# A written-out order of operations replaced by another one, in an attention and MLP-mixer kernel

## The chip, the cores and the metric

One core of one Trainium2 chip. The metric is the device time of one execution in microseconds (us). Each core has five engines with instruction queues of their own: TensorE (PE in the profile; its weight loads are listed as PEld), VectorE (DVE), ScalarE (ACT), GpSimd (POOL) and SyncE (SP). Transfers (DMAs) are issued from such a queue and run on the core's 16 DMA engines.

## What is computed

Sliding-window attention with a linear bias, whose output goes through an MLP-mixer layer. Shapes: q, k, v are (8, 8, 576, 64), the output is (8, 576, 512), all float32.

```python
# attention: B = 8, H = 8, S = 576, D = 64, window 128
scores = scale * np.matmul(q, k.transpose(0, 1, 3, 2))
rel = pos[:, None] - pos[None, :]
mask = (rel >= 0) & (rel < window)
scores = np.where(mask, scores + bias[None], -1000000000.0)   # bias: -slope(head) * |rel|
attn = softmax(scores)
x = np.matmul(attn, v)          # -> (8, 576, 512), heads side by side
# mixer: d_tok = 256, d_ch = 1536
h = np.maximum(x.transpose(0, 2, 1) @ w_tok1, 0.0) @ w_tok2
u = x + h.transpose(0, 2, 1)
h2 = np.maximum(u @ w_ch1, 0.0) @ w_ch2
out = u + h2
```

## The kernel before

**Tiling.** A sequence of 576 rows is four blocks of 128 and a rest of 64. Two batches form a pair; their rests share one tail block (block 8; blocks 0 to 3 are the first batch's, 4 to 7 the second's). Data is bfloat16 on the chip, float32 in the accumulators and in the output. All weights stay on the chip.

**Stages of a block and of a batch**, with the lines by which the profile names them:

- *Loads.* `load` (line 596) issues from POOL one transfer with conversion to bfloat16 per block and tensor, into rings of five `qk` and five `v` buffers. The tail block has two per tensor, one for each batch.
- *Turns.* q and k must stand with the head dimension on the partitions. `transposes` does that on PE (line 754, copied out at line 760) for the first pair's blocks and by a DMA transpose from SP (line 743) for the others, into a ring of seven `qkT` buffers.
- *Scores.* Matmuls of line 791, exp on ACT (line 806), mask multiplication on DVE (line 816). *Values:* matmuls of line 871 with a column of ones for the row sums, reciprocal on DVE (line 901), normalization on DVE (line 904) or ACT (line 909).
- *Token mix* (lines 933 to 994): two products with the token weights and the residual; the result `ub` is turned on PE for the first three batches and by SP's DMA transposes (line 1002) for the later ones.
- *Channel mix.* The first product is direct (line 1491) for batches 0 to 2 and in seven partial products (line 1391) for batches 3 to 7. Some of these seven are kept in float32 in buffers of the ring `ob` (named `raw` or `ob` in the profile; copy on ACT, line 1406, or on DVE, line 1407), later added to another product (line 1415) and cut at zero (DVE, line 1417, or ACT, line 1419). DVE prepares differences of the inputs at line 1354. The tail block has a direct product (line 1534).
- *Second product of the channel mix* (line 1668), again in seven partial products; the evictions (line 1639) add the residual into `ob` buffers, and line 1651 stores each finished quarter of a batch: from SP, but for batches 5 and 6 from POOL. The tail blocks have a product of line 1579, an eviction (line 1586) and two stores (line 1595).

While PE does the channel mix of batch b, the attention and the token mix of batch b + 1 run between its products: the kernel is one stream in which the stages of two batches are woven together.

**What sets the order.** The functions named above do not emit instructions. Each makes an operation (`Plan.op`) with its engine, its dependencies and the buffers it makes and uses; 1528 operations in all. Three constants written out at the head of the file then say what becomes of them, and `Plan.follow` reads them:

- `ORDER` (line 343): the numbers of the operations in base 36, in one sequence. Each engine executes its own operations in this sequence; there is no other priority.
- `ELSEWHERE` (line 388): operations that can run on ACT or DVE and are to run on the other one than their default.
- `PLACES` (line 391): for each buffer, in the order of first use, the slot of its ring (for `ps`, the PSUM bank). An operation that takes over a slot waits for all users of the slot's previous buffer.

```python
ops, seq = self.ops, [self.ops[number(x)] for x in ORDER.split()]
...
for x in ELSEWHERE.split():
    o = ops[number(x)]
    o.eng, o.cost, o.emit = o.other
line = {e: [o for o in seq if o.eng == e] for e in ("PE", "ACT", "DVE", "POOL", "SP")}
...
places = iter(PLACES)
for o in seq:
    for b in o.bufs:
        if b.slot is None:
            first = number(next(places))
```

The rest of `follow` only guesses times, by which `emit` sorts the operations (engine by engine this is the sequence of `ORDER`) and puts small matmuls of zeros (line 1726) into PE's guessed gaps of the first 60 us. The queues are in order: an instruction that waits holds all that stand behind it on its engine. POOL's queue holds the loads, one pause (line 1025, a small copy that waits for a turned block of batch 4) and the late stores; SP's holds both kinds of turns and the other stores.

Of the kernel before, what the change touches and what calls it, by code (L numbers as in the profile page):

```python
# [70 lines left out]
class Plan:  # L71
# [60 lines left out]
    def follow(self):  # L132
        def number(x):
            return int(x, 36)

        ops, seq = self.ops, [self.ops[number(x)] for x in ORDER.split()]
        assert sorted(o.n for o in seq) == list(range(len(ops)))
        for x in ELSEWHERE.split():
            o = ops[number(x)]
# [5 lines left out]
        for o in ops:  # L145
            for d in o.deps:
                succ[d].append(o)
        places = iter(PLACES)
        for o in seq:
# [134 lines left out]
    def emit(self, spin):  # L284
# [20 lines left out]
        for _, _, go in sorted(work, key=lambda w: w[:2]):  # L305
# [37 lines left out]
ORDER = ("h i 4z f j g 52 k d e 0 l 59 7 1 2 8 4v m 3 4 4x n 4w 9 4y o a 55 5 41 50 42 56 43 53 57 44 51 p 58 54 5c q "  # L343
# [44 lines left out]
ELSEWHERE = ("4w 4y 56 5m 63 6i 71 74 82 86 8a a1 a5 b4 b6 c1 c3 ct cz fb fo ft fw gh gj gn gp gr gt gv h7 j0 j2 jk jw ku "  # L388
             "l5 ls lu m0 n8 na of oo op oz qa qd qq qv qy sl t3 t6 th uc uf uh us vd vi vn wv y0 y2 z5 zx 10a 10f 125 12m "
             "12p 130 13n 13q 144 14e 14h 14w 154")  # L390
PLACES = ("000232243674016170016710104526473452324062714260014501022423400510303647106542202567210123732010446005172042"
          "362051274206715214600503123154312004710320646027513140700140215467140010640713055567102605442020611541127230"
          "025262104700230014425051403512010500312141045110243012320140672042576220135742000764034632027316250001410345"
          "032144211356403132100450246021001275130420276110007602714237320407630130523116201136100600423450014031202753"
          "010221310424602240716150473245124022651103414372613403103250016362440743151304001632203241351701025422040305"
          "000654201226422044020117553524030170503214160073144603151242005002361430470201452220764207205106323324401126"
          "21054020440646533020470006402521147105523572030164250114")
UNIT_LATE = False
SECOND_LATE = False
GATE = True  # L400
# [1360 lines left out]
```

## Time and profile before

| | us |
|---|---|
| runs of the kernel | 274.78, 274.56, 272.98 |
| median of them | 274.56 |
| the profiled execution's own time | 274.01 |
| its span on the core | 272.1 |
| granted TensorE clock | 1.00 |

The profile shows one execution. The span runs from the first to the last recorded activity; the profiled execution's own time is 1.9 us longer. "Busy" is the time that an engine spends in instructions; the matmuls' ends are modelled, and those of consecutive matmuls overlap, so distances from start to start are the safer measure of PE's pace. A wait is written as the instruction that waited and, behind the arrow, what came last before it could go, with the total, the number and the longest of such waits. In timeline rows the first two columns are start and length in us, and a wait that ended with the row's start stands in brackets. Of a DMA the row on POOL or SPq is the issue alone; a source view gives the time from issue to landing.

### The profile page before, as it was taken

The page shows a single profiled execution, that of the slowest core. Times are in us where ns is not written, and L with a number is a line of the kernel's source. Part 1 is how long each engine was busy: PE and PEld are TensorE (multiplying, and loading weights), DVE is VectorE, ACT ScalarE, POOL GpSimd, SP SyncE. Part 2 cuts the span into 40 slices and gives each one's busy share as a digit, 9 for nine tenths or more (in the row PEclk, how much of TensorE's full clock was granted, in tenths as well). Part 3 has the DMA queues.
Part 4 walks back from the last instruction along what each step waited for, and adds up shares of the span by engine and source line. Part 5 has one row for each costly group of instructions (what it writes and reads, how often), then busy time and mean ns, then how long its engine had stood idle before and what let it go on. Part 6 is the DMA issues. An engine that isn't in the chain of part 4 may idle for free.

```text
span 272.1 us, 7520 instructions
## 1 busy us (share of the span) xinstructions
PE 263.2 (97%) x3033; PEld 195.6 (72%) x3033; DVE 234.0 (86%) x533; ACT 159.5 (59%) x306; POOL 114.8 (42%) x147
## 2 busy tenths in 40 slices
PE   7989999999999999999999999999899989999994
PEld 5767565776686656588877876688776768588883
DVE  7886598983996799889999899999899989987992
ACT  6974787144963469229991299428881379413900
POOL 8987977640680866601680137400740410003000
PEclk9999999999999999999999999999999999999999
DMA  8999999999999999999999899979999430044006
GB/s 197 179 170 181 150 191 183 149 111 181 190 142 169 176 139 230 161 116 232 80 177 149 221 141 78 124 183 164 147 165 111 129 107 2 12 88 149 8 0 193
DMA packets 160338, 38.59 MB, mean 142 GB/s; under 512 B 146544, under 2 KB 159472, under 8 KB 160304
## 3 DMA queue, kind: packets, MB, share of 16 engines
q0 software_dynamic: 109968, 19.64, 90.3%
q1 hardware_dynamic: 49104, 17.70, 33.9%
q10 hardware_dynamic: 1232, 0.79, 1.0%
q8 instruction: 23, 0.38, 0.6%
q14 instruction: 11, 0.09, 0.1%
HBM read 35.85 MB, written 9.44 MB: 166 GB/s over the span
## 4 chain that ended last, share of the span: by engine, by line
PE 71%; DMA 11%; issue 7%; DVE 5%; POOL 4%; ACT 1%; SPq 0%; POOLq 0%; DVEq 0%
PE ps L1668 24%; PE ps L1391 11%; PE ps L1491 11%; PE ps L871 5%; PE ps L933 4%; PE ps L976 4%; PE ps L791 3%; DMA qk<-in_k_dram 3%; PE ps L1534 3%; PE ps L1579 3%; DMA v<-in_v_dram 2%; DMA qkT<-qk 2%; DMA W<-in_moe_w_tok_dram 2%; POOL qk L596 2%; DVE r L1415 2%
## 5 line engine op out<-in xcount | busy, mean ns | idle before, releaser
L806 ACT ACTIVATE pe<-ps 128x1024 bf16<-128x1024 f32 (+1 forms) x56 | 51.8, 971 | 15.8 <-PE ps L791 15.8
L596 POOL DMA_DIRECT2D qk<-in_k_dram x35 | 29.9, 868 | 52.2 <-DMA qkT<-qk 49.0
L596 POOL DMA_DIRECT2D v<-in_v_dram x36 | 30.9, 867 | 30.8 <-PE ps L871 29.9
L1668 PEld LDWEIGHTS <-r 128*128 128x128 bf16 x384 | 36.6, 98 | 8.0 <-issue 1.3
L596 POOL DMA_DIRECT2D qk<-in_q_dram x35 | 30.3, 875 | 11.4 <-DMA qkT<-qk 7.6
L816 DVE TENSOR_TENSOR pe<-pe,mask 128x1024 bf16<-128x1024 bf16 (+1 forms) x48 | 30.3, 647 | 3.4 <-ACT pe L806 3.2
L1491 PE MATMUL ps<-uT,WC 128*128 128x512 bf16 x132 | 32.0, 379 | 0.0
L1406 ACT COPY raw<-ps 128x512 f32<-128x512 f32 x32 | 19.0, 596 | 21.8 <-PE ps L1391 11.9
L1668 PEld LDWEIGHTS <-s 128*128 128x128 bf16 x288 | 27.7, 98 | 5.2 <-issue 0.4
L909 ACT ACTIVATE xb<-ps,rt 128x64 bf16<-128x64 f32 x80 | 18.3, 324 | 19.2 <-DVE rt L901 19.1
L1415 DVE TENSOR_TENSOR r<-ps,raw 128x512 bf16<-128x512 f32 x37 | 24.6, 679 | 1.8 <-PE ps L1391 1.7
L1391 PE MATMUL ps<-tt,WS 128*128 128x256 bf16 x180 | 25.9, 273 | 0.0
L1668 PE MATMUL ps<-WC,r 128*128 128x256 bf16 x192 | 25.7, 273 | 0.0
L1391 PEld LDWEIGHTS <-WS 128*128 128x128 bf16 x240 | 21.9, 98 | 4.9 <-issue 1.2
L871 PEld LDWEIGHTS <-pe 128*128 128x128 bf16 (+1 forms) x480 | 20.4, 99 | 6.5 <-issue 1.4
L1668 PE MATMUL ps<-WT,r 128*128 128x256 bf16 x192 | 24.7, 273 | 0.0
L1668 PE MATMUL ps<-WT,s 128*128 128x256 bf16 x192 | 24.1, 273 | 0.0
L871 PE MATMUL ps<-v,pe 128*128 128x65 bf16 (+1 forms) x480 | 23.0, 194 | 0.6 <-ACT pe L806 0.3
L994 DVE TENSOR_TENSOR ub<-ps,xb 128x512 bf16<-128x512 f32 x32 | 21.0, 683 | 2.9 <-PE ps L976 2.7
L1497 ACT ACTIVATE r<-ps 128x512 bf16<-128x512 f32 x26 | 15.1, 613 | 10.0 <-PE ps L1491 8.7
L1639 DVE TENSOR_TENSOR raw<-ps,ub 128x512 f32<-128x512 f32 x27 | 18.3, 683 | 2.1 <-PE ps L1668 2.1
L1491 PEld LDWEIGHTS <-WC 128*128 128x128 bf16 x132 | 11.6, 98 | 11.8 <-issue 0.2
(145 smaller groups left out, 519.1 us busy)
## 6 DMA issues: line engine op xcount, KB each, us to landing
out_dram<-raw SPq DMA_DIRECT2D x19, 256.0 KB, 2.6
qk<-in_q_dram POOLq DMA_DIRECT2D x30, 128.0 KB, 4.9
qk<-in_k_dram POOLq DMA_DIRECT2D x30, 128.0 KB, 4.9
v<-in_v_dram POOLq DMA_DIRECT2D x28, 128.0 KB, 5.6
WC<-in_moe_w_ch_dram POOLq DMA_DIRECT2D x8, 384.0 KB, 7.6
out_dram<-raw POOLq DMA_DIRECT2D x8, 256.0 KB, 2.8
out_dram<-ob SPq DMA_DIRECT2D x5, 256.0 KB, 2.6
v<-in_v_dram POOLq DMA_DIRECT2D x16, 64.0 KB, 4.8
```

What stands on the lines that cost most here:

```text
L596: nc.gpsimd.dma_start(out=to()[p0 : p0 + n, :, :], in_=rows(src, b, s0, n))
L806: act_.activation(out=pb()[:, e, :, lo:, c0:c1_], in_=wide(e)[:, :, lo:, c0:c1_], func=ACT.Exp, scale=scale)
L816: dve_.tensor_tensor(out=o, in0=o, in1=heads(mk, es), op=ALU.mult)
L871: pe_.matmul(view(e)[a:z, i, :], lhsT=pb()[:, e, i, kind, a:z], rhs=vb()[:, HEADS[e][i], 0 : D + 1], start=start, stop=stop, skip_group_ch ...
L909: act_.activation(out=x4()[:, i, :], in_=view(e)[r0:r1_, i, 0:D], func=ACT.Copy, scale=rt()[r0:r1_, 0, i, :])
L994: plan.op("DVE", 690, lambda blk=blk, ht=ht, hs=hs: dve_.tensor_tensor(out=ub()[:, blk, :], in0=ht()[:, hs], in1=xb()[:, blk, :], op=ALU.a ...
L1391: pe_.matmul(bk()[:, c * HS : (c + 1) * HS], lhsT=l(c, cb), rhs=r(cb), start=new and c == 0 and cb == 0, stop=cb == 1, skip_group_check=True)
L1406: return plan.op("ACT", 600, lambda: act_.copy(out=e()[:, :], in_=bk()[:, :]), rk + UNIT_RANK, makes=e, uses=[bk], other=("DVE", 690, lamb ...
L1415: add = plan.op("DVE", 690, lambda: dve_.tensor_tensor(out=o(), in0=half_of(bk), in1=half_of(e), op=ALU.add), rk + UNIT_RANK, uses=[bk, e] ...
L1491: pe_.matmul(ct()[:, :], lhsT=WC1[:, cb, t * P : (t + 1) * P], rhs=uT()[:, cb, :], start=cb == 0, stop=cb == NCB - 1)
L1639: dve_.tensor_tensor(out=v, in0=bk().rearrange("p (c n) -> p c n", c=2), in1=src, op=ALU.add)
L1668: pe_.matmul(bk()[:, c * HN : (c + 1) * HN], lhsT=l(t, c), rhs=w(t), start=first, stop=g == 1 and t == HK - 1, skip_group_check=True)
```

## The change

The three constants get new contents; nothing else in the file is changed. The operations, their number, shapes and dependencies, and the constants of the time guess are the same. What differs:

- Every engine's sequence, behind a common beginning: the first 132 operations of `ORDER` are the same. PE's sequence is the same for its first 39 operations of 546, ACT's for 24, DVE's for 48, POOL's for 25 of 142, SP's for 3 of 80.
- 73 operations change between ACT and DVE (`ELSEWHERE` has 71 entries for 80, of which 39 are common). DVE has 525 operations of the sequence for 518, ACT 235 for 242.
- The slots of most buffers, and with them what each operation waits for when it takes over a slot.
- On POOL, the pause goes from place 136 (counted from 0) to 121, between loads; the store 1177 (base 36: wp), one of the two tail stores of line 1595 for batches 4 and 5, goes from place 131 to 139, behind the stores 1158, 1162, 1170, 1176, 1333, 1166 and 1337; the load 105 (base 36: 2x; v of the tail block, batch 5's rows) goes from place 83 to 97, behind the loads 99, 116 and 112.

```diff
@@ -343,58 +343,58 @@
 ORDER = ("h i 4z f j g 52 k d e 0 l 59 7 1 2 8 4v m 3 4 4x n 4w 9 4y o a 55 5 41 50 42 56 43 53 57 44 51 p 58 54 5c q "
...
-         "6w 13 6t 73 6r 6x 74 79 6u 14 6y 75 17 6z 76 7g 7a 7b 7h 70 77 7c 78 7d 9k 7i 71 7j 7k 7e 7r 9l 7f 9m 9p 9q "
-         "7u 7q 7t 7s 7l 7w 7v 7y 9n 9o 7m 9z 7x 81 9y 84 a2 a0 80 7z 9r 85 a1 83 a3 9s 9t 1b 18 1a 15 7o 7p 19 7n 89 "
...
+         "6w 13 6t 73 6r 6x 74 79 6u 14 6y 75 7g 6z 7h 7a 70 9k 76 7i 7b 77 7j 78 71 7c 7d 9l 7k 9m 9p 9q 7s 7l 7r 7q "
+         "17 18 7m 9n 1a 7e 7f 7v 7u 9z 7t 7w 7y 81 7z 7x 9o 80 83 84 87 9r 1b 15 88 82 9s 85 9y a2 a3 a0 a1 86 9t 89 "
...
-ELSEWHERE = ("4w 4y 56 5m 63 6i 71 74 82 86 8a a1 a5 b4 b6 c1 c3 ct cz fb fo ft fw gh gj gn gp gr gt gv h7 j0 j2 jk jw ku "
-             "l5 ls lu m0 n8 na of oo op oz qa qd qq qv qy sl t3 t6 th uc uf uh us vd vi vn wv y0 y2 z5 zx 10a 10f 125 12m "
-             "12p 130 13n 13q 144 14e 14h 14w 154")
-PLACES = ("000232243674016170016710104526473452324062714260014501022423400510303647106542202567210123732010446005172042"
...
+ELSEWHERE = ("4w 4y 56 5m 63 6i 71 74 7b 7m 86 8q 9l b6 bb bz c1 c5 c9 cb cr cx cz f9 fb fo fv fw g6 gl gp gv h7 hb j0 j2 "
+             "km ko kr ku la n8 na p0 pl pw qa qq qv qy sl t3 t6 th u7 uh us uy y0 y2 y7 z8 zp zu 10a 10f 10i 125 13s 13v "
+             "14w")
+PLACES = ("003212240671046170016740104526373452324062714260014501042433400570301705144201675412010323107004216257003205"
...
```

More of the change, by code (lines that the diff above doesn't have):

```diff
@@ L345 @@
          "x 6v 5u 5r y 6j 5s 46 47 66 72 6k 5v z 6a 48 6b 10 6d 6l 6g 6e 6h 6f 67 6m 6c 68 6i 11 69 6n 6p 6o 12 6s 6q "
[42 rows of a table removed]
-ELSEWHERE = ("4w 4y 56 5m 63 6i 71 74 82 86 8a a1 a5 b4 b6 c1 c3 ct cz fb fo ft fw gh gj gn gp gr gt gv h7 j0 j2 jk jw ku "
-             "l5 ls lu m0 n8 na of oo op oz qa qd qq qv qy sl t3 t6 th uc uf uh us vd vi vn wv y0 y2 z5 zx 10a 10f 125 12m "
-             "12p 130 13n 13q 144 14e 14h 14w 154")
-PLACES = ("000232243674016170016710104526473452324062714260014501022423400510303647106542202567210123732010446005172042"
[L392 to L397, printed above, removed]
[42 rows of a table added]
+ELSEWHERE = ("4w 4y 56 5m 63 6i 71 74 7b 7m 86 8q 9l b6 bb bz c1 c5 c9 cb cr cx cz f9 fb fo fv fw g6 gl gp gv h7 hb j0 j2 "
+             "km ko kr ku la n8 na p0 pl pw qa qq qv qy sl t3 t6 th u7 uh us uy y0 y2 y7 z8 zp zu 10a 10f 10i 125 13s 13v "
+             "14w")
+PLACES = ("003212240671046170016740104526373452324062714260014501042433400570301705144201675412010323107004216257003205"
+          "641706352202725436005436271105033000632630072410114040701502140104714220342304025413021700643022546250220341"
+          "316722102002453010102056421503214205044213503412142022014465200647300501206520720320651564073003452034231504"
+          "123150160456024213530400205370161045200207106212764027040722074415601215301003427210710320050367121221141152"
+          "031204314046302240761104124027041261500143322167424013000734201410253146012040745500304100413360215420055637"
+          "425520732103302341220256234551132067120051007012416711240203160736445202005105632206027406203712324234311047"
+          "01520301572402234060205700120114533267304510405207532164")
 UNIT_LATE = False
```

80 rows, old and new, of the table ORDER are left out of this document.

## The prediction

> **What bounds the kernel now.** I read the page's totals first, then busy time by stretch, then TensorE's waits after the opening, then the timeline around each wait.
>
> ```profile
> span 272.1 us, 7520 instructions
> PE 263.2 (97%) x3033; PEld 195.6 (72%) x3033; DVE 234.0 (86%) x533; ACT 159.5 (59%) x306; POOL 114.8 (42%) x147
> ```
>
> The stretches (columns: length, then PE, PEld, DVE, ACT and POOL busy with counts, granted clock, DMA share, GB/s):
>
> ```profile
> 0.00:20.00 20.00, 17.45 (x297) 13.11 (x297) 16.61 (x60) 15.13 (x28) 17.36 (x28) 1.00 1.43 182
> 20.00:60.00 40.00, 39.65 (x448) 26.27 (x447) 32.56 (x74) 24.01 (x48) 29.30 (x37) 1.00 1.90 161
> 60.00:160.00 100.00, 100.00 (x1121) 71.06 (x1119) 85.47 (x189) 60.54 (x117) 44.27 (x53) 1.00 1.52 166
> 160.00:170.00 10.00, 9.38 (x130) 6.90 (x128) 9.80 (x26) 9.97 (x21) 5.06 (x7) 1.00 1.44 114
> 190.00:200.00 10.00, 9.27 (x159) 8.43 (x157) 9.05 (x23) 8.95 (x14) 5.98 (x7) 1.00 1.56 145
> 200.00:220.00 20.00, 19.88 (x190) 14.21 (x189) 18.40 (x41) 7.75 (x19) 6.79 (x10) 1.00 1.03 143
> 220.00:240.00 20.00, 19.15 (x208) 14.19 (x208) 19.57 (x46) 13.36 (x27) 0.00 (x0) 1.00 0.09 26
> 260.00:272.10 12.10, 8.45 (x78) 7.34 (x75) 6.94 (x13) 0.00 (x0) 0.00 (x0) 1.00 0.34 108
> ```
>
> TensorE is the bound: at full clock it is busy for 263.2 of 272.1 us. Of the idle 8.9 us, 2.55 are in the opening (20.00 − 17.45) and 3.65 in the last stretch, mostly the evictions and stores behind the last matmul. What an order can win in between is 0.35 + 0.62 + 0.73 + 0.12 + 0.85 = 2.67 us shown. Every wait of TensorE that the profile lists after 20 us:
>
> ```profile
> PE ps L1391 <- DVE raw L1407: 0.9, 1, 0.9
> PE ps L791 <- DMA qkT<-qk: 0.7, 1, 0.7
> PE ps L754 <- DMA qk<-in_k_dram: 0.3, 1, 0.3
> PE ps L871 <- ACT pe L806: 0.3, 1, 0.3
> PE ps L871 <- DVE xb L904: 0.2, 1, 0.2
> ```
>
> So loads, turns (DMA transposes) and stores each stop TensorE once, and two waits are for the elementwise engines around 160 to 170, where DVE is busy for 9.80 and ACT for 9.97 of 10 us. The two long ones:
>
> ```profile
> 160.67 0.41 PE L871 MATMUL ps<-v,pe 128*128 128x65 bf16 x8
> 161.01 0.23 PE L791 MATMUL ps<-qkT 64*128 64x128 bf16 x2
> 186.19 0.22 PE L791 MATMUL ps<-qkT,qkT 64*128 64x128 bf16 x2
> 187.43 1.76 SPq L743 DMA_TRANSPOSE qkT<-qk  x1
> 191.22 0.41 PE L871 MATMUL ps<-v,pe 128*128 128x65 bf16 x8
> 191.85 0.89 POOL L596 DMA_DIRECT2D qk<-in_k_dram  x1 [18.69 <-DMA qkT<-qk]
> 192.36 0.23 PE L791 MATMUL ps<-qkT 64*128 64x128 bf16 x2 [0.73 <-DMA qkT<-qk]
> DMA to landing us min/median/max: 3.1/3.6/8.3
> ```
>
> (The last line is line 743's.) A values group of eight matmuls is followed by scores after 0.34 us where nothing waits (160.67 to 161.01), and after 1.14 us at 191.22: 0.80 is lost, 0.07 more than the idle shown, as the modelled end of a matmul covers part of a gap.
>
> ```profile
> 167.00 0.28 PE L871 MATMUL ps<-v,pe 128*128 128x65 bf16 x4
> 167.12 0.82 PE L1668 MATMUL ps<-WC,r 128*128 128x256 bf16 x6
> 214.27 0.56 POOL L1595 DMA_DIRECT2D out_dram<-ob  x1 [10.75 <-DVE ob L1586]
> 215.57 4.37 DMA out_dram<-raw
> 219.15 0.61 PE L1391 MATMUL ps<-tt,WS 128*128 128x256 bf16 x4
> 219.59 0.28 PE L871 MATMUL ps<-v,pe 128*128 128x65 bf16 x4
> 220.03 0.69 DVE L1407 COPY raw<-ps 128x512 f32<-128x512 f32 x1 [1.03 <-DMA out_dram<-raw]
> 220.78 0.60 PE L1391 MATMUL ps<-uT,WS 128*128 128x256 bf16 x4 [0.90 <-DVE raw L1407]
> DMA to landing us min/median/max: 2.2/2.7/5.4
> ```
>
> (The last is line 1651's.) This chain reads: POOL's queue stands 10.75 us at a store of line 1595 whose data is late, two stores of line 1651 behind it leave only at 214.83 to 215.57, the second lands 4.37 us later, and the copy of line 1407 into the same buffer starts then. TensorE starts 1.19 us after the four matmuls at 219.59; in an even place 0.12 (167.00 to 167.12). Loss: 1.07. Four matmuls of line 1391 shown as 0.61 take 0.44 (219.15 to 219.59), so a gap can hide up to 0.17.
>
> **The change part by part.** Operations, shapes and the matmuls' count stay, so TensorE's 263.2 us of work stays. The first 132 operations are the same ones in the same order: the opening's 2.55 stays. I laid the last 60 operations of both orders side by side; the chain matmul, eviction, store keeps its length, so the tail's 3.65 stays.
>
> (a) *Turns.* The transpose that was late at 192.36 left SyncE at 187.43. In the new order its buffer is given free by the scores that end at 186.41 (186.19 + 0.22), so it can leave then; and one product (0.44) moves into the stretch before its user. Window: 191.22 − 186.41 + 0.34 + 0.44 = 5.6 us, against 4.93 (192.36 − 187.43) from issue to use last time and landings of 3.1/3.6/8.3. At the time measured here it is in time: −0.80; but seven loads now stand at this place on POOL, where the old order's came only from 191.85 on. The worst landing, 8.3, would be 2.7 late, +1.9 net. I take −0.6. Behind this scores group on TensorE stand all later matmuls, so a lateness goes into the end in full.
>
> (b) *Stores.* The store of line 1595 goes from place 131 of POOL's list to 139, behind six stores of line 1651 and the other store of line 1595, so those seven no longer stand behind its 10.75 us. They leave as soon as their data is there; if that is only 1.03 us sooner, the copy at 220.03 finds its buffer free: −1.07 at most, 0 if the store is held by its own data. Against it: in the new order another keep (line 1406) takes over one of those buffers, and between the eviction that fills it and that keep stand two groups of line 1668 (0.82 − 0.17 each), three of line 1391 (0.44) and one of eight values matmuls (0.41 − 0.16), 2.9 us, which the landing of 2.2/2.7/5.4 about meets. Two products and a scores group (some 0.5) follow before TensorE needs the keep, 1.4 us, so only landings beyond about 4.3 count. I take −0.9.
>
> (c) *Shares of ACT and DVE.* 73 operations change engine; DVE goes from 518 listed operations to 525. In the tight stretch one keep goes ACT to DVE, one relu DVE to ACT and one ACT to DVE.
>
> ```profile
> L1406 ACT COPY raw<-ps 128x512 f32<-128x512 f32 x32 | 19.0, 596 | 21.8 <-PE ps L1391 11.9 <-DVE tt L1354 9.8
> L1419 ACT ACTIVATE r<-r 128x512 bf16<-128x512 bf16 x21 | 12.7, 637 | 0.8 <-DVE r L1415 0.8
> L1417 DVE TENSOR_SCALAR r<-r 128x512 bf16<-128x512 bf16 x24 | 8.0, 349 | 0.1
> ```
>
> (us, mean ns.) The relus cancel (0.64 and 0.35 each way); the keep takes 0.60 from ACT and, by the copy at 220.03, adds 0.69 to DVE. Two waits of 0.3 and 0.2, with 0.17 hidden at each, are 0.8 of loss here, and with the two other gaps that the 0.62 holds some 1.2. Bounds: −1.2 if relieving ACT clears all, +0.7 if DVE, full already, is late by the whole copy. Midway: −0.2.
>
> (d) *Loads early.* Loads of the second and third batch leave POOL 2 to 20 us sooner, as their buffers come free sooner. The wait for a load at line 754 (0.35 with 0.17 hidden: 0.5) shrinks, since the transposes that wait come some 0.7 us of matmul work later (a chunk of line 1491 is moved ahead of them, a values group behind) while the load keeps its place on POOL: −0.4, from 0 to −0.5. Elsewhere TensorE waits for no load, so earlier loads win nothing; their cover is 100.00 of 100.00 us of matmuls from 60 to 160.
>
> (e) *One load late.* One load goes the other way: the second half of a v tail block (batch 5's rows), which left at 104.7, moves from place 83 of POOL's list to 97, behind three loads, the first of which waits for the values at 127.95 to free its buffer.
>
> ```profile
> 127.95 0.88 POOL L596 DMA_DIRECT2D v<-in_v_dram  x1 [14.37 <-PE ps L871]
> 135.45 0.53 PE L871 MATMUL ps<-v,pe 128*128 128x65 bf16 x12
> DMA to landing us min/median/max: 3.4/4.9/9.4
> ```
>
> (The last is line 596's.) Its user are the last four of the twelve matmuls at 135.45, so at about 135.70; the new order has one matmul of line 933 more before it (0.2). From 127.95 to 135.9 less three issues of 0.88 leaves 5.3 us from issue to use, against landings of 3.4/4.9/9.4. At the median it costs nothing, at worst 4.1. I take +0.3.
>
> In TensorE's queue nothing can pass a wait, so all these lie on the path. Sum against the profiled execution's own 274.01: 274.0 − 0.6 − 0.9 − 0.2 − 0.4 + 0.3 = **272.2 us**. That execution lies 0.55 under the median of 274.56; I leave the number as it is. About 1% (2.7 us) is what a measurement of this kernel can tell from no change, so the forecast's own gain of 1.8 against the execution, 2.4 against the median, lies inside it.
>
> **The rivals.**
>
> *Stalls only move: 274.0.* The total of matmul work is the same, and with DVE at 18.40 of 20 and 19.57 of 20 from 200 to 240 any reorder can be late somewhere else. For it: (a) to (c) have bounds on both sides. Against it: the two long waits have named causes that the new order takes away. New stalls of 1.8 would take up the gain.
>
> *Every stall after the opening goes: 269.7.* 2.67 shown and some ten gaps (I count them in the timeline) with about 0.16 hidden in each: 274.0 − 4.3. For it: loads, turns and stores all get wider windows nearly everywhere. Against it: one place with full DVE and ACT.
>
> *Slower: the late v load decides.* Place and price as in (e). From a landing above 5.3 us on, TensorE stands at the tail block's values, with all else queued behind. At 9.4: 4.1, with the other gains 272.2 − 0.3 + 4.1 = 276.0; with none, 278.1. For it: the load shares the engines with two loads issued in the two microseconds before. Against it: median 4.9.
>
> *Loads disturb turns: 273.7.* With seven loads issued right behind the transpose of (a), its packets share the DMA engines with theirs. If that doubles 3.6 to 7.2, it misses the 5.6 window by 1.6: in place of −0.6 stands +0.8 (1.6 less the 0.80 that goes), so 272.2 + 1.4 = 273.6; with a little lateness elsewhere I say 273.7. For it: landings up to 8.3 were seen. Against it: the median, with loads about nearly everywhere, is 3.6. The Trainium skill, page "DMA: Bandwidth & Descriptors", in the section on queues, rings and completion order, says that each engine takes turns between the queues that have work for it, a packet at a time, which is this rival's mechanism; the trace's 8.3 fits it, its median of 3.6 speaks against a doubling as the rule.
>
> **How the numbers follow.** Forecast 272.2: 0.40 (its own range 270.9 to 273.5). Stalls only move, 274.0: 0.22. All gone, 269.7: 0.18. Late v load, 276.0: 0.10. Loads against turns, 273.7: 0.10. Range 269.6 to 276.2: it reaches from the rival without stalls to the late load. Faster by over 1% means under 271.8, slower over 277.3: faster has the case without stalls (0.17 of it) and 0.15 of the forecast's own lower end, 0.32; slower has the upper part of the late load and of chains of lateness that I did not find, 0.13; same 0.55.
>
> **What the profile after would show.** (a) right: no wait of line 791 on qkT near 190; wrong: one of over 0.3 us. (b) right: POOL's wait at line 1595 no longer has stores of line 1651 behind it, and line 1391 does not wait for a copy near 219. (c) right: TensorE idle from 160 to 170 below 0.4; DVE's total some 1 to 3 us above 234.0. (d) line 754's wait below 0.2. (e) wrong: a wait of line 871 on the DMA of v near 134. As a whole, TensorE's idle time between 20 and 260 us should fall from 2.67 to about 1.2. A sum over 2.5 there, or a changed opening or tail, would make the prediction wrong.

## The result and the profile after

The changed kernel takes 272.3 us in the median of 16 runs (271.26 to 274.19), the kernel before 274.51 us in 16 runs on the same chips; the ratio is 0.9937, with a 95% interval of 0.9912 to 0.9963. The forecast was 272.2. The profiled execution has 272.05 us of its own time and a span of 270.3 us, 1.8 less than before. One of the twelve executions of b_two_shift below took 673.4 us; it is left out of that kernel's ratio, and nothing on record says what held it.

Page and stretches of the kernel after (same columns as before):

```profile
span 270.3 us, 7524 instructions
PE 263.4 (97%) x3033; PEld 195.2 (72%) x3033; DVE 236.0 (87%) x540; ACT 154.9 (57%) x287; POOL 114.6 (42%) x147
```

```profile
0.00:20.00 20.00, 17.84 (x298) 13.20 (x298) 16.57 (x60) 15.29 (x29) 17.18 (x28) 1.00 1.39 180
20.00:60.00 40.00, 40.00 (x444) 26.54 (x443) 32.37 (x73) 22.73 (x42) 30.41 (x38) 1.00 1.97 173
60.00:160.00 100.00, 99.36 (x1122) 70.43 (x1121) 88.94 (x195) 57.37 (x106) 45.01 (x53) 1.00 1.53 160
160.00:170.00 10.00, 9.63 (x133) 7.16 (x130) 9.97 (x28) 10.00 (x23) 1.41 (x2) 1.00 1.28 155
190.00:200.00 10.00, 10.00 (x169) 8.62 (x168) 9.75 (x26) 9.44 (x16) 6.42 (x8) 1.00 1.46 94
200.00:220.00 20.00, 20.00 (x189) 14.42 (x188) 18.06 (x40) 8.53 (x22) 5.06 (x7) 1.00 0.92 144
220.00:240.00 20.00, 20.00 (x229) 15.19 (x226) 19.23 (x44) 13.42 (x25) 0.00 (x0) 1.00 0.12 28
260.00:270.30 10.30, 6.62 (x61) 5.68 (x59) 4.55 (x9) 0.00 (x0) 0.00 (x0) 0.97 0.36 112
```

TensorE's waits after 20 us, all that the view lists:

```profile
PE ps L1391 <- DMA uT<-ub: 0.4, 1, 0.4
PE ps L1391 <- DVE r L1415: 0.3, 1, 0.3
PE ps L1668 <- DVE s L1516: 0.2, 1, 0.2
```

All five waits of before are gone. Idle time between 20 and 260 us is 0.64 + 0.37 = 1.01 us for 2.67; 0.64 of what is left stands between 60 and 160, where before had none, and most of the rest near 163. The last stretch keeps its idle time (10.30 − 6.62 = 3.68 for 3.65). The opening reads 2.16 idle for 2.55, but nothing was won there: the last matmul of the common beginning starts at 22.60 us for 22.64.

Wherever both kernels have started the same set of matmuls, their times can be compared directly; the difference is the lead of the kernel after. It is 0.04 us at 27.4 (time of before), 0.56 at 31, 0.74 at 121, −0.36 at 160, −0.03 at 190, 0.77 at 192, 1.66 at 222, 1.84 at 234 and 1.83 at the last matmul. So the 1.8 us come from:

| us | change of TensorE's loss | part of the prediction |
|---|---|---|
| 20 to 31 | −0.5 | (d), −0.4 |
| 31 to 110 | −0.2 | not foreseen |
| 110 to 160 | +1.1 | not foreseen; (e), +0.3, was near 135 |
| 160 to 190 | −0.3 | (c), −0.2 |
| 190 to 200 | −0.8 | (a), −0.6 |
| 200 to 222 | −0.9 | (b), −0.9 |
| 222 to 240 | −0.2 | not foreseen |
| all others | 0.0 | 0.0 |

The places of the terms in the kernel after: the transpose of (a), the scores that use it, the load of (e) with its user, and the store and keeps of (b) with a product near them. The transpose's own landing stands in the view of transfers for the 1 us in which it was issued.

```profile
184.35 3.10 SPq L743 DMA_TRANSPOSE qkT<-qk  x2
191.59 0.23 PE L791 MATMUL ps<-qkT 64*128 64x128 bf16 x2
...
130.31 0.72 POOL L596 DMA_DIRECT2D v<-in_v_dram  x1
135.68 0.29 PE L871 MATMUL ps<-v,pe 128*128 128x65 bf16 x4
...
214.46 0.73 POOL L1651 DMA_DIRECT2D out_dram<-raw  x1 [1.71 <-DVE raw L1639]
217.05 1.07 ACT L1406 COPY raw<-ps 128x512 f32<-128x512 f32 x2 [0.63 <-PE ps L1391]
218.38 0.60 PE L1391 MATMUL ps<-tt,WS 128*128 128x256 bf16 x4
```

```profile
qkT<-qk SPq DMA_TRANSPOSE x1, 4.6
v<-in_v_dram POOLq DMA_DIRECT2D x1, 64.0 KB, 4.9
out_dram<-raw POOLq DMA_DIRECT2D x1, 256.0 KB, 2.6
```

The transpose left at 186.03 (the second of the two in the row), landed after 4.6 and was needed at 191.59: 0.9 us in hand. The load left at 130.31, landed after 4.9 and was needed at 135.68: 0.45 in hand, from a window of 5.4 us. The store left at 214.46, landed after 2.6, and the second keep in the row (217.53) took its buffer 0.45 us later. Three terms, none with a wait, all within a microsecond of one.

### The profile page after: what moved, and what is told of

It reads as the page before. It is cut to its first block, busy times and chain, and to the rows that moved or that the text cites. A ratio compares the mean times of both kernels' runs of the same rounds, so it can differ in the third digit from the quotient of the medians.

```text
span 270.3 us, 7524 instructions
## 1 busy us (share of the span) xinstructions
PE 263.4 (97%) x3033; PEld 195.2 (72%) x3033; DVE 236.0 (87%) x540; ACT 154.9 (57%) x287; POOL 114.6 (42%) x147
## 4 chain that ended last, share of the span: by engine, by line
PE 84%; DMA 6%; DVE 5%; issue 1%; SPq 1%; ACT 1%; POOL 0%; POOLq 0%; DVEq 0%
PE ps L1668 24%; PE ps L1391 17%; PE ps L1491 11%; PE ps L871 6%; PE ps L791 5%; PE ps L933 4%; PE ps L1534 4%; PE ps L976 3%; PE ps L1579 3%; DMA v<-in_v_dram 2%; DMA W<-in_moe_w_tok_dram 2%; DMA uT<-ub 2%; DVE ub L994 1%; SPq L1002 1%; DVE s L1516 1%
## 5 line engine op out<-in xcount | busy, mean ns | idle before, releaser
L1406 ACT COPY raw<-ps 128x512 f32<-128x512 f32 x36 | 20.7, 612 | 39.8 <-PE ps L1391 37.9
L1668 PEld LDWEIGHTS <-s 128*128 128x128 bf16 x288 | 27.4, 98 | 6.9 <-issue 1.1
L1415 DVE TENSOR_TENSOR r<-ps,raw 128x512 bf16<-128x512 f32 x39 | 26.1, 683 | 2.7 <-PE ps L1391 2.0
L871 PEld LDWEIGHTS <-pe 128*128 128x128 bf16 (+1 forms) x480 | 19.4, 99 | 5.8 <-issue 0.7
L871 PE MATMUL ps<-v,pe 128*128 128x65 bf16 (+1 forms) x480 | 22.3, 194 | 0.1
L909 ACT ACTIVATE xb<-ps,rt 128x64 bf16<-128x64 f32 (+1 forms) x64 | 14.8, 344 | 12.1 <-DVE rt L901 12.0
L904 DVE TENSOR_TENSOR xb<-ps,rt 128x256 bf16<-128x256 f32 (+1 forms) x48 | 19.8, 419 | 0.8
```

What stands on the lines that cost most here:

```text
L871: pe_.matmul(view(e)[a:z, i, :], lhsT=pb()[:, e, i, kind, a:z], rhs=vb()[:, HEADS[e][i], 0 : D + 1], start=start, stop=stop, skip_group_ch ...
L904: dve_.tensor_tensor(out=x4(), in0=view(e)[r0:r1_, :, 0:D], in1=rt()[r0:r1_, 0, :, :].broadcast_to([r1_ - r0, 4, D]), op=ALU.mult)
L1406: return plan.op("ACT", 600, lambda: act_.copy(out=e()[:, :], in_=bk()[:, :]), rk + UNIT_RANK, makes=e, uses=[bk], other=("DVE", 690, lamb ...
L1415: add = plan.op("DVE", 690, lambda: dve_.tensor_tensor(out=o(), in0=half_of(bk), in1=half_of(e), op=ALU.add), rk + UNIT_RANK, uses=[bk, e] ...
L1668: pe_.matmul(bk()[:, c * HN : (c + 1) * HN], lhsT=l(t, c), rhs=w(t), start=first, stop=g == 1 and t == HK - 1, skip_group_check=True)
```

## The experiments

All times are compared by their ratio to the kernel before on the same chip. Names that begin with b_ change the kernel before, those with a_ the kernel after. The first ones ask whether the sum's terms are what the prediction said; they leave a question open, and the last four answer it. Two theories ran through all of them: that a stall of TensorE is local, so that what is taken away comes off the end; and that stalls only move.

**b_store: the tail store behind the others.**

```diff
 POOL (operation numbers)
-141 1177 1158 1162 1176 1166 913 1170 1337
+141 1158 1162 1176 1166 913 1170 1177 1337
```

> The kernel before with one operation moved: the tail store 1177 (line 1595) on POOL goes behind the stores 1158, 1162, 1176, 1166 and 1170. Theory (each stall of TensorE is local, and taking it away brings the end forward by its size): the wait of line 1391 on the copy of line 1407 near 219.6 (1.07 us) goes, nothing of that size comes in its place; about 273.4 us where before has 274.5. Rival (with VectorE full there, the gain is given back a little later): the wait goes, others of together about 1 us appear between 220 and 260, and the time stays at 274.5.

Ratio 1.0009 (0.998 to 1.0038): no gain. The profile near 219:

```profile
215.26 0.73 POOL L1651 DMA_DIRECT2D out_dram<-raw  x1 [2.98 <-DVE raw L1639]
219.48 0.69 DVE L1407 COPY raw<-ps 128x512 f32<-128x512 f32 x1 [0.41 <-DMA out_dram<-raw]
220.22 0.60 PE L1391 MATMUL ps<-uT,WS 128*128 128x256 bf16 x4 [0.28 <-DVE raw L1407]
215.26 4.13 DMA out_dram<-raw
```

The store is no longer behind line 1595, but it leaves only 0.3 us sooner than before (215.57), as now its own data is last; and it still takes 4.13 us to land. 0.6 of the 1.07 us went at this place. In the same execution other waits stood in place of those of before (0.5 for a qkT near 66, 0.5 for a load of v near 83), ahead of anything that the edit moves: which transfer is late differs from one execution to the next. The opening differs too: the same scores (line 791) start at 30.42 us in after, at 29.86 in a_store and at 31.48 in a_load, whose orders are the same up to there. So single spans are compared less surely than the distances within a trace.

**b_two: store and transpose.**

```diff
 POOL: as in b_store
 SP
-1190 1076 993 1215 997 1202 1001
+1190 1076 1202 993 1215 997 1001
```

> The kernel before with two operations moved: the store as in b_store, and on SyncE the transpose 1202 ahead of the store 993, two transfers earlier than its old place. Theory: both long waits go (1.07 near 219.6, 0.80 to 0.89 near 191.2), so some 1.9 us less than before, 272.6 us; two moves would then win as much as the whole rewriting (272.3). Rival: one or both are replaced by other waits; 273.4 to 274.5.

Ratio 0.9989 (0.9967 to 1.001). The transpose left at 184.33 and the wait at 191 is gone (0.80 from start to start); the three transfers ahead of it in SyncE's queue had been enough to hold it, for its landing, 4.84 us, was no shorter (4.88 before). But the store took 4.5 us, and the product near 219 waited more than in b_store:

```profile
214.38 0.73 POOL L1651 DMA_DIRECT2D out_dram<-raw  x1 [2.98 <-DVE raw L1639]
219.73 0.60 PE L1391 MATMUL ps<-uT,WS 128*128 128x256 bf16 x4 [0.67 <-DVE raw L1407]
out_dram<-raw POOLq DMA_DIRECT2D x1, 256.0 KB, 4.5
```

So two moves did not win as much as the rewriting.

**b_apart: are neighbouring stores to blame?**

```diff
 POOL
-141 1158 1162 1176 1166 913 1170 1177 1337
+141 1158 1162 1166 913 1170 1176 1177 1337
```

> As b_two, and the store 1176 (line 1595) also goes behind the store 1170 on POOL, so that of the stores behind 1162 only 1166, 1.7 us later, leaves while 1162 is under way. In b_two the store 1162 left at 214.38 and took 4.52 us with two stores behind it; in the kernel after it took 2.62 alone. Theory (stores that leave within two microseconds of each other slow each other, and that, not the place behind the waiting store, makes the copy of line 1407 wait): 1162 lands in 2.6 to 3.4 us, the wait of line 1391 on line 1407 (0.7 in b_two) goes below 0.2, and the time is 0.5 to 0.8 us under b_two's. Rival (the landing is long here for another reason): above 4 us, wait and time as in b_two.

The store landed in 4.40 us with no other store issued for 1.7 us, and line 1391 waited 0.56: the theory of neighbours falls for this store. Ratio 0.9975 (0.9947 to 1.0003), by which it can't be told from b_two.

**a_store: the tail store put ahead again.**

```diff
 POOL
-1158 1162 1170 1176 1333 1166 1337 1177
+1158 1177 1162 1170 1176 1333 1166 1337
```

> The kernel after with the tail store 1177 (line 1595) put on POOL ahead of the store 1162, as soon as its data is computed. Theory: the store 1162 leaves at about 217.3 in place of 214.5 and lands at about 219.7, the keep of line 1406 that takes over its buffer waits from 217.5 to then, and TensorE's product behind it is late by 1 to 2 us; 273.3 to 274.3 us. Rival (the cover of 1.4 us between keep and product, and slack behind it, swallow it): below 0.4 us, 272.3 to 272.7.

```profile
216.25 1.43 POOL L1651 DMA_DIRECT2D out_dram<-raw  x2
218.93 0.58 ACT L1406 COPY raw<-ps 128x512 f32<-128x512 f32 x1 [2.40 <-DMA out_dram<-raw]
219.57 0.60 PE L1391 MATMUL ps<-tt,WS 128*128 128x256 bf16 x4 [2.13 <-ACT raw L1406]
220.68:224.09 3.41, 3.41 (x39) 2.44 (x37) 2.22 (x6) 2.55 (x4) 0.00 (x0) 0.50 0.01 2
```

Ratio 1.003 (1.000 to 1.006), about 2.5 us over the kernel after. In the profile 2.3 us are lost at this product, and 1.3 more behind it (6.14 us from there to the scores at 225.71, in after 4.84). There TensorE waits for nothing (3.41 us busy of 3.41 in the last line); its granted clock is 0.50 for these 3.41 us, from 1.1 us behind the late product on. Six of the twelve executions have a mean clock of 0.991 to 0.993, and they are the six longest (274.44 to 277.01 us, the others 273.65 to 274.34). The only other profile here with such a stretch inside the kernel is b_shares', 0.50 for 3.41 us from 155.29 on, 0.8 us behind a wait of 1.87; waits of up to 1.5 us in the other profiles, and one of 2.6 in b_shares, have none behind them, so what brings it on is open. The place of this store does decide in the order of after. The landing, though, was 2.58 here with a store 0.55 ahead and another 0.72 behind.

**a_load: the late load, later by two.**

```diff
 POOL
-99 116 112 105 111 130 117
+99 116 112 111 130 105 117
```

> The kernel after with the v load 105 put two loads later on POOL, behind the loads 111 and 130. In the profile of after it landed at 135.23 for a user at 135.68. Theory (the predicted slower rival: from a window of some 5.3 us on, its landing decides): it leaves at about 133.1, lands at 136.5 to 138.0, line 871 waits 0.8 to 2.3 us on the transfer of v, and the time is longer by as much, about 273.8 us. Rival (the queue of DMAs makes up for a late issue, or TensorE's lateness is made good later): wait and difference below 0.4 us, 272.3 to 272.7.

```profile
134.03 0.71 POOL L596 DMA_DIRECT2D v<-in_v_dram  x1
138.16 0.28 PE L871 MATMUL ps<-v,pe 128*128 128x65 bf16 x4 [1.30 <-ACT raw L1406]
v<-in_v_dram POOLq DMA_DIRECT2D x1, 64.0 KB, 4.0
```

The load landed at 138.0 and its user started at 138.16, 1.47 us later relative to the rest. The view puts the wait to line 1406, which came last by its semaphores; the landing shows the load. Ratio 1.0004 (0.9978 to 1.003), 1.8 us over after. The slower rival's mechanism, its place and the point from which it decides are as predicted; the kernel after stands 0.45 us from it.

**a_shares and b_shares: order and engine shares apart.** In a_shares the kernel after has ELSEWHERE of before; in b_shares the kernel before has ELSEWHERE of after.

> The kernel after with the engine shares of before: 73 operations go back to the other of ACT and DVE, at their new places in the order. Theory of the prediction (shares are worth about 0.2 us): 272.0 to 273.0 us, TensorE's waits on DVE and ACT after 20 us in sum under 1.0. Rival (shares and order belong together: an order made for other shares leaves an engine late): waits of together 1.5 to 4 us, 274 to 276 us.

> The kernel before with the engine shares of after, order and slots as before. Theory: within 0.5 us of before, the two waits between 160 and 170 (0.3 and 0.2) change by less than 0.5 in sum. Rival (belonging together): 1.5 to 4 us slower by new waits on DVE or ACT.

Ratios 1.0377 (1.0335 to 1.042) and 1.0759 (1.0718 to 1.0799), 12 and 21 us over their originals; both theories were far too low. Busy times hardly change:

```profile
PE 267.1 (95%) x3047; PEld 198.0 (70%) x3072; DVE 232.8 (83%) x533; ACT 160.4 (57%) x306; POOL 115.1 (41%) x147
```

(a_shares; its 283.5 us also hold some 40 more filler matmuls, which the kernel puts into guessed gaps.) DVE is no busier than in before, which has the same shares: 232.8 for 234.0. So it is waiting, not work: TensorE's longest waits in a_shares are for DVE at lines 1516 (1.6 us in two waits) and 1407 (1.5 us). I take it that an operation that changes engine comes into a queue whose sequence belongs to the other shares and waits there behind work that is not ready; that was not tried by itself.

**a_fix: mend the waits of after.**

```diff
 PE
-654 736 840 740    828 805 811 807    950 1038 1039
+654 840 736 740    828 811 805 807    950 1039 1038
 DVE
-1025 1023 948
+1025 948 1023
```

> The kernel after with four exchanges of neighbours where its profile shows waits of TensorE: the scores 840 ahead of the product 736 (near 121, wait for a turn, 0.60 from start to start), the product 811 ahead of 805 (near 147, wait for a sum, 0.37), on DVE the join 948 ahead of the mask 1023 and on TensorE the values 1039 ahead of 1038 (near 163, wait for a join, 0.47). Theory (stalls are local, what is taken away comes off the end): about 1.0 us less than after, 271.3 us against 272.3, and the three waits gone. Rival (they move): 272 to 272.6, other waits of the same sum.

Ratio 0.9959 (0.9939 to 0.9979): no gain. Here the rival holds. Near 121 the scores filled TensorE's gap, but then products came later than before to the engines behind them:

```profile
121.25 0.23 PE L791 MATMUL ps<-qkT 64*128 64x128 bf16 x2
125.41 0.60 PE L1391 MATMUL ps<-uT,WS 128*128 128x256 bf16 x4 [0.18 <-ACT raw L1406]
```

Of the 0.6 us that the first exchange could win, 0.1 is left at 126 us; of the 0.4 near 147 nothing is left at 153; and between 163 and 173 some 0.5 is lost, where DVE's order was changed: in after, DVE and ACT are busy for 9.97 and 10.00 of 10 us from 160 to 170.

**What makes one landing 2.6 and another 4.5?** What moved while the store was under way, by queue: the late one of b_two (214.3 to 217.5 us; it landed at 218.90), then the prompt one of after (214.4 to 216.6). q0 is POOL's queue, q1 SyncE's; the profile calls the kind of q8 and q14 "instruction".

```profile
q0 software_dynamic: 121, 0.38, 38.7%
q8 instruction: 1, 0.02, 3.3%
q14 instruction: 1, 0.01, 0.9%
```

```profile
q1 hardware_dynamic: 852, 0.21, 51.8%
q0 software_dynamic: 75, 0.26, 35.2%
```

In b_two a packet of q8 lies in the store's flight; in after the next one starts at 216.64, just as the store's last packets end (216.67). In before one lies in the store's flight too (217.3) and one at 187.1, in the flight of the transpose just ahead of the late one on the same queue (it landed after 5.9 us), and in after one at 118.8, in that of the late turn. Each is 16 KB and takes 0.9 to 1.9 us. The page of after counts 24 of them, one for about 250 of TensorE's 6066 matmuls and weight loads: together with their kind, they look like fetches of its instructions. If so, the number of TensorE's instructions in the opening sets where they fall. The last four kernels cut the opening's filler matmuls into smaller ones over the same columns (the edit for 41 more; a_hit has 11e3 for 30e3, and 14 more):

```diff
-        work += [(a, -1, lambda i=i, m=m, n=n: spin(i, m, n)) for a, i, m, n in fills]
+        work += [(a, -1, lambda i=i, m=m, n=n, a=a: spin(i, m, n, WARM <= a < 30e3)) for a, i, m, n in fills]
...
-    def spin(bank, wide, narrow):
-        for n in [DM] * wide + [P] * narrow:
+    def spin(bank, wide, narrow, split=False):
+        for n in [R] * (2 * narrow) if split else []:
+            pe_.matmul(bank[:, 0:n], lhsT=zero[:, 0:P], rhs=zero[:, 0:n], start=True, stop=True)
+        for n in [P] * (4 * wide) if split else [DM] * wide + [P] * narrow:
```

> The kernel before, order untouched; the filler matmuls of zeros from 7 to 19 us are cut into smaller ones over the same columns, 41 more matmuls and as many weight loads. The profiles show on queue q8 a packet of 16 KB about every 256 instructions of TensorE (in before at 187.1 and 217.3, taking about 1 us); 82 more instructions bring each forward, by the counts to about 184 and 213.3. Theory (a transfer with such a packet in its flight lands 1.4 to 2 us later, and the two long waits of before come from that): the transpose 1202 lands in 3.2 to 3.9 us in place of 4.88, the store 1162 in 2.6 to 3.3 in place of 4.37, the waits at 191 and 219 go or fall below 0.3 each; 272.9 to 273.5 us where before has 274.5, ratio 0.993 to 0.997. Rival (the landings come from place and neighbours in the queues): both waits as before, ratio 1.000.

> The kernel after with the same cut of the fillers. Packets of q8 would lie at about 114.5, 185.2 and 212.5 in place of 118.8, 187.6 and 216.6. Theory: the turn 727 (117.07, landed in 4.39) lands in 2.4 to 3.2, the wait at 121 (0.60 from start to start) goes; 271.7 against 272.3, ratio 0.991 to 0.994. Rival: 0.994, wait as in after.

> b_two with the same cut. Theory: the store 1162 lands in 2.6 to 3.3 us in place of 4.52, the wait of line 1391 on the copy of line 1407 (0.7 in b_two) goes; 0.5 to 0.9 us under b_two, ratio 0.995 to 0.997. Rival: landing above 4 us, ratio as b_two, 0.999.

> The kernel after with only the fillers from 7 to 11 us cut, 28 more instructions of TensorE: by the counts packets of q8 at about 186.9 and 215.5, that is into the flights of the transpose 1202 (issued at 186.0, 0.94 us of margin in after) and of the store 1162 (issued at 214.5, landed in 2.62, 0.45 us of margin). Theory: 1162 lands in 4.0 to 4.6 us, the keep of line 1406 and the product behind it are late by about 1 to 1.5 us, 1202 lands in 4.5 to 5.9 us and is late by up to 0.7; 273.3 to 274.5 us, ratio 0.997 to 1.000. Rival: landings as in after, ratio 0.994.

The packets moved: in b_shift to 183.2 and 215.1, in a_shift to 113.5, 181.3 and 212.2, in a_hit to 117.5, 184.1 and 215.3, within 4 us of the counts. First a_shift (ratio 0.9917, 0.9885 to 0.995) and a_hit (0.9961, 0.9938 to 0.9985), the same order in both. The turn of line 1002 at 117.67 and the product behind it in a_shift, then the store, keep and product in a_hit:

```profile
uT<-ub SPq DMA_TRANSPOSE x1, 2.4
120.90 0.60 PE L1391 MATMUL ps<-uT,WC 128*128 128x256 bf16 x4
```

```profile
q8 instruction: 1, 0.02, 3.2%
213.96 4.69 DMA out_dram<-raw
q0 software_dynamic: 5, 0.02, 5.6%
218.75 0.58 ACT L1406 COPY raw<-ps 128x512 f32<-128x512 f32 x1 [1.61 <-DMA out_dram<-raw]
219.39 0.60 PE L1391 MATMUL ps<-tt,WS 128*128 128x256 bf16 x4 [1.34 <-ACT raw L1406]
```

With the packet away, the turn lands in 2.4 for 4.4 and the wait at 121 is gone (0.6, and 0.6 off the span: 269.7). With the packet in it, the store lands in 4.69 for 2.62 and the product is 1.5 us late. The packets' own times show how: the q8 packet runs from 215.34 to 217.21; 60 of the store's 64 packets of 4 KB are through by 216.2, and then nothing of POOL's queue moves until 217.19, when the last four follow, one after another (the line of five packets is the view of 217.1 to 218.25, the fifth a small one). No packet of q14 lies in this flight. TensorE's starts in after, a_shift and a_hit agree to 0.01 us from 30 to 120 us; behind the store a_hit is 1.5 us later than a_shift, of which 0.1 stood at 121 already. The medians differ by 1.3 us (271.89 and 273.2), and seven of the eight runs of a_shift lie below all twelve of a_hit. The transpose 1202 was not hit in a_hit, as the packet came at 184.1 and not at 186.9, and landed in 3.5.

b_two_shift (0.996, 0.9934 to 0.9987): the store lands in 2.6, the wait near 219 is gone, and the ratio is the expected one, though its interval still overlaps that of b_two. In b_shift (0.9978, 0.995 to 1.0007) less came than the 0.993 to 0.997 expected, and its profile shows why:

```profile
186.24 0.58 ACT L1406 COPY raw<-ps 128x512 f32<-128x512 f32 x1 [1.97 <-DMA out_dram<-raw]
186.88 0.60 PE L1391 MATMUL ps<-uT,WS 128*128 128x256 bf16 x4 [0.48 <-ACT raw L1406]
```

The wait at 191 went (0.80) and that at 219 fell from 0.90 to 0.45 as the view counts it, but the packet now lay at 183.2, in the flight of a store on SyncE (4.2 us, in before 2.5), and the keep that takes its buffer came late: 0.65 lost at 186.9, in b_two_shift 0.51. The store near 219 landed in 3.9 in b_shift, not in 2.6 to 3.3; there it stands between stores 0.7 us away on both sides, and half of the cause is open.

Over the ten profiles of these kernels with little changed and the two of before and after, from 40 us on: the stores of line 1651 with a q8 packet that starts 0.3 to 2.3 us after their issue land in 4.05 us (median of 52), those with none from 2 us before to 6 us behind in 2.59 (142). For the transposes of line 743 it is 4.70 (63) and 3.24 (100), for the turns of line 1002 3.94 (41) and 2.39 (84), for the loads 4.98 (197) and 4.56 (349). These medians only go together with the packets; that the packets make the delay is shown at the places above, where they were moved.

## Why the prediction was right, and where it was not

The time was right, and the sum's terms stand in the table above at their places with nearly their sizes; idle time between 20 and 260 us fell to 1.01, where about 1.2 was forecast. But the causes were only partly those named, and that the sum hit is in part luck: the four gains came to 2.5 us for 2.1, (e) cost nothing for 0.3, 0.4 of gains was not foreseen, and a loss of 1.1 that was not foreseen took up just that.

*(a) Turns.* Right in place, in size and in what lets the transpose go: the scores that free its buffer end at 186.00 and it leaves at 186.03; its window (5.6 us forecast) is 5.56 (186.03 to 191.59). Of the old lateness I named neither cause: its place on SyncE behind stores (b_two), and a q8 packet in the flight of the transpose ahead. Changing the place alone was enough, with a landing of 4.62 us and not the 3.6 that I counted on; in b_shift, with the place left and the packet away, it landed in 3.9 us for 4.88 and the wait was gone as well.

*(b) Stores.* The size was right, the cause half wrong. I gave the wait to the stores' late start behind line 1595 and took the 4.37 us of landing as it was. Against TensorE the store hardly starts sooner in after: 3.92 us ahead of the product at 218.38, for 3.58 ahead of the one at 219.15, since its own data is late, the case that I had put at 0. b_store took line 1595 away and won 0.6 of 1.07 in place and nothing in time, since the landing stayed above 4 us; b_two_shift took away the packet and the wait went. In the new order the q8 packet comes when the store is through, and the keep that takes over the store's buffer starts only at 217.53. That the packet comes then is luck: in a_hit, with the same order and 14 more matmuls in the opening, it does not. The risk named there, the other keep that takes over the store's buffer with an even window, is real: a_hit and a_store make it pay 1.5 and 2.3 us.

*(c) Shares.* −0.3 for −0.2, with the wrong idea of what the term is. Costed as durations of 73 operations, shares are worth tenths; put into the other kernel's order, 12 to 21 us. The bounds of −1.2 and +0.7 hold for this pair of order and shares only.

*(d) Loads.* −0.5 for −0.4. The size of this one varies: in b_store, with the order of before, the wait at line 754 was not there either.

*(e) The late load.* 5.4 us of window for 5.3, a landing of 4.9 like the median that I went by, and no wait. a_load shows the rival's price: with a window of 2.7 us and a landing of 4.0, 1.5 us.

*What was missed* is the 1.1 us between 110 and 160: the turn at 121, whose four transposes follow each other on SyncE's queue from 113.07 to 118.28 with the last block's landing late by a q8 packet (a_shift takes 0.6 away), a sum at 147 that DVE finishes 0.4 late, and some token-mix groups. The prediction had asked which waits of before go and which transfers leave later; these were in time before, and nothing of them was moved by name. The rival "stalls only move" has thus its part: 2.9 us went, 1.1 came. The rival "every stall goes" fell with that 1.1. The rival "loads disturb turns" was not put to the test at its place: its seven loads were to leave right behind the transpose of 186.03, but POOL waited until 190.42, and the transpose landed at 190.65.

```profile
190.42 1.77 POOL L596 DMA_DIRECT2D qk<-in_k_dram  x2 [15.47 <-DMA qkT<-qk]
```

At the places that were late, q8 packets lay in the flights; but the landing of 8.3 itself (issued at 47.97) had none in its flight, and no run moved the loads away from a turn, so what they cost elsewhere is open. The Trainium skill, page "DMA: Bandwidth & Descriptors", section on queues, rings and completion order, has an engine take turns between queues packet by packet; the trace of a_hit agrees, for one packet of 16 KB takes 1.87 us there, and the last four packets of the store, which landed 2.07 us later than in after, follow right behind it.

## What to carry to other kernels

In a hand-written order, a late transfer has a place and a landing, and they want separate proof: move the transfer and look whether its landing changes, before the gain is promised. Give transfers whose landing is waited for some 2 us over their quiet time (here 2.6 for a store, 3.2 for a transpose), since something will lie in the flight of one of them. Shares of engines and order are one decision; a gain from filling one gap of TensorE is only real where the engines that feed the next product have room.

## What the runs showed of the hardware

The packets on q8, fetches of TensorE's instructions as it seems (16 KB for about 250 of them, 0.9 to 1.9 us each), hold up the data transfers that they meet: the store near 215 landed in 4.1 to 4.7 us with one in its flight, in 2.6 to 2.8 without in after, a_store, a_shift and b_two_shift, but in 3.9 without in b_shift. With the same order, 14 or 41 more matmuls in the opening made 0.9961 or 0.9917 of before, by where those packets fall. A cut of fillers, of all edits, gave the fastest kernel measured here (a_shift, 271.89 us); against the kernel after, 0.9917 and 0.9937, it can't be told apart. Behind a wait of TensorE of about 2 us the granted clock was 0.50 for 3.41 us in two profiles (a_store, b_shares), in a_store at a price of 1.3 us.
